# An attention backward core: q loads issued singly, the output scaled by GpSimd after one copy, and its fp32 transposes at full width

## Chip, cores and metric

The kernel runs on one core of a Trainium2 chip. The metric is the device time of one execution in microseconds (us); a kernel's figure is the median of its runs.

Engine names are those of the profile: PE is the TensorE matmul, PEld its weight load, DVE is VectorE, ACT is ScalarE, POOL is GpSimd. SP is the sync engine, which only issues DMAs here.

## The reference, cut to what matters

Two attention blocks share the input size (2048 tokens, 448 features, 16 heads of 28). Block A is linear attention, block B is softmax attention with 16 query heads over one shared k and v. The kernel returns the concatenated output and all eight gradients.

```python
def _B_ref(x, wq, wk, wv, wo):            # 16 heads, Dh = 28
    q = (x @ wq).reshape(B, S, H, Dh).transpose(0, 2, 1, 3)
    k = x @ wk
    v = x @ wv
    scores = jnp.einsum("bhqd,bkd->bhqk", q, k) * (Dh ** -0.5)
    p = softmax(scores, axis=-1)
    o = jnp.einsum("bhqk,bkd->bhqd", p, v)
    return o.transpose(0, 2, 1, 3).reshape(B, S, H * Dh) @ wo
...
def reference(A_x, ..., B_wo, grad_out):
    _out, _vjp = jax.vjp(_f, A_x, A_wqkv, A_wo, B_x, B_wq, B_wk, B_wv, B_wo)
    return (_out, *_vjp(grad_out))
```

The change touches block B alone: its forward and backward pass, which the kernel runs together in one loop.

## The kernel before

The loop, called the attention core here, has 64 blocks (a chunk of 256 queries of two heads) of 8 units (256 keys each), so 512 units. In unit u the PE makes the scores of unit u and dP of unit u-16; ACT makes two exponentials of 512 columns and one copy (`cp`) of half of dP; the DVE makes the first half of dS (`dst[:, 0, :]`) and a 32x32 transpose (`dsx`); POOL makes the other half (`dst[:, 1, :]`). A unit's number modulo 8 is its place. Once a block there is extra work for the output o:

- Place 1: the DVE copies the unnormalised o, transposed, from PSUM (`oTs`).
- Place 2: the PE transposes it into the spare PSUM bank (`onat_T`); DVE and POOL work on it (`o_norm`). Row 0 of each head holds the sum of the exponentials, so its reciprocal `rl` is one over the softmax denominator.
- Place 4: `row_D` puts sum(dO * o) into column 0 of `don`, the scaled dO.
- Place 6: the PE transposes `don` (`don_T`), again into the spare bank. From then on dP of the next block can be made.

```python
def onat_T(b, bank):
    onp = bank[:, 0:P].rearrange("p (q h c) -> p q h c", q=2, h=2)
    for qb in range(2):
        for j in range(4):
            mmt(bank[32 * j:32 * j + 32, qb * 64:qb * 64 + 64], oTs[:, qb * P + 32 * j:qb * P + 32 * j + 32],
                identF[:, 0:64], (0, 32 * j), True, True)
    onps[b] = onp

def o_norm(b):
    # ... onp, r_ (the new rl), os_ (a view of oTs), dnv (do_nat of this block)
    nc.vector.reciprocal(out=r_[:], in_=onp[:, :, :, 0:1])
    nc.vector.tensor_tensor(out=os_, in0=onp[:, :, :, :], in1=r_[:].to_broadcast([P, 2, 2, 32]), op=ALU.mult)
    # ... new tiles prod and dn (= don[b])
    nc.gpsimd.tensor_tensor(out=prod[b][:], in0=dnv, in1=os_, op=ALU.mult)
    nc.gpsimd.tensor_tensor(out=dn[:], in0=dnv, in1=r_[:].to_broadcast([P, 2, 2, 32]), op=ALU.mult)
    nc.gpsimd.tensor_copy(out=dnv, in_=os_)

def row_D(b):
    Dq = pw_.tile([P, 2, 2, 1], F32, name="Dq")
    nc.vector.tensor_reduce(out=Dq[:, :, :, 0], in_=prod[b][:], axis=AX.X, op=ALU.add)
    nc.gpsimd.tensor_tensor(out=don[b][:, :, :, 0:1], in0=Dq[:], in1=rl[b][:], op=ALU.mult)

for u in range(NU + 28):                  # NU = 512
    spare = ...                           # the score bank that unit u does not use
    rows_SD(u, sp, dp)                    # scores of u, dP of u-16
    if (b := due(u, 10)) is not None:     # place 2
        onat_T(b, spare)
    if (b := due(u, 14)) is not None:     # place 6
        don_T(b, spare)
    # ... exponential, dst[:, 0, :] on the DVE, cp on ACT, dst[:, 1, :] on POOL
    for a in {10: (0, 2), 18: (1, 3)}.get(u, ()) or {38: (0, 2), 54: (1, 3)}.get(u % 64, ()) * (u < 448):
        # ... qX[qc]: the next q chunk, a quarter (32 partitions, 256 KB) by each load
        nc.gpsimd.dma_start(qX[qc][32 * a:32 * a + 32, :, :, :]..., qn_d[qc * 256:(qc + 1) * 256, :]...)
    if u == 44:
        nc.gpsimd.dma_start(wo, ...)
    if (b := due(u, 12)) is not None:     # place 4
        row_D(b)
    # ... place 2: o_norm(b); place 6: don_copy(b); second exponential; products; dsx
```

POOL carries out its instructions in this order, so a q load issued in a unit stands ahead of `o_norm` and `row_D` of the same unit.

## Time and profile before

| | before |
|---|---|
| median of 3 runs, us | 1084.57 (1081.98 to 1086.64) |
| span of the profiled run, us; clock | 1083.6; 0.995 |
| PE, DVE, ACT, POOL busy, share of the span | 95%, 83%, 81%, 71% |
| up to the core, core (first exponential of unit 0 to that of unit 511), after it, us | 221.5, 785.5, 76.6 |
| median unit, us: place 2; place 4 (even, odd blocks); place 6 (even, odd) | 1.733; 1.596, 1.480; 1.480, 1.526 |
| median unit of an odd place, us | 1.447 |

A unit's time is read from the ACT timeline: from the start of its first exponential to that of the next unit's. The medians are over units 128 to 447, where nothing but the loop runs. I call what a unit takes above the median of its place (even and odd blocks apart) a stall, where it is over 0.1 us. Sums of stalls run over units 16 to 510 and leave out place 0, which takes 0.2 to 0.3 us more below unit 128 and from 448 on because other work falls there. Before, the stalls sum to 12.2 us.

A few more lines of before matter later. The first is from the costliest groups on the page (engine, operation, shapes, count, busy us, mean ns, idle time ahead), the second from the groups by shape between 400 and 1000 us:

```profile
L640 PE MATMUL sps<-identF,oTs 128*32 128x64 f32 x1024 | 27.6, 225 | 7.3
```
```profile
L792 POOL CAST R<-oTs 128x128 bf16<-128x128 f32 x49 | 14.2, 289 | 3.1
```

The 8 transpose products of a block are 16 MATMULs in the record (1024 in 64 blocks), and POOL's conversion of o to bf16 takes 289 ns. The waits of the PE in the core (total us, times, longest us):

```profile
PE dk_acc L640 <- issue: 3.8, 1, 3.8
...
PE sps L805 <- POOL don L797: 0.8, 1, 0.8
```

The transposes of `don` (L805) waited for POOL a single time, and the one long stall was an "issue", which is time in which the engine waited for nothing that the profile shows.

### The profile page before, as it was taken

The numbers are of one execution on the slowest core, as the hardware profiler recorded it, in microseconds if no ns is written. First come the engines' busy times: TensorE is split into PE (matmuls) and PEld (weight loads), VectorE is DVE, ScalarE is ACT, GpSimd is POOL, SyncE is SP. The second block draws the span as 40 slices with busy tenths as digits, with TensorE's granted clock in tenths as the row PEclk, the third lists the DMA queues.
The fourth block names the chain that finished last, engine by engine and source line by source line (L and its number), as shares of the span: only waits on it lengthen the run. The fifth ranks groups of instructions, "written<-read, shape, count | busy, mean of one in ns | idle before, by whom it ended". The sixth has DMA issues, their size and how long they took to land.

```text
span 1083.6 us, 41908 instructions
## 1 busy us (share of the span) xinstructions
PE 1033.1 (95%) x17222; PEld 502.1 (46%) x17225; DVE 896.5 (83%) x1790; ACT 873.4 (81%) x1743; POOL 772.4 (71%) x1014
## 2 busy tenths in 40 slices
PE   9999999999989999999999999999999999999998
PEld 5555555444434444444444444444444444444444
DVE  7896400439979999999999999999999999999942
ACT  6453122579979999999999999999999999999621
POOL 6001243328877888889889988988988898888881
PEclk9999999999999999999999999999999999999999
DMA  9879899399999999999999999999999999999973
GB/s 240 165 134 193 171 189 202 69 219 198 198 177 196 165 202 181 202 189 200 190 185 194 194 193 193 200 186 186 189 205 186 188 191 202 183 167 188 223 141 89
DMA packets 669033, 199.47 MB, mean 184 GB/s; under 512 B 646008, under 2 KB 664736, under 8 KB 668840
## 3 DMA queue, kind: packets, MB, share of 16 engines
q1 hardware_dynamic: 656296, 175.23, 96.8%
q0 software_dynamic: 7584, 17.59, 6.9%
q10 hardware_dynamic: 4960, 3.96, 1.3%
q8 instruction: 135, 2.21, 0.9%
q14 instruction: 58, 0.48, 0.1%
HBM read 20.99 MB, written 12.94 MB: 31 GB/s over the span
## 4 chain that ended last, share of the span: by engine, by line
PE 37%; ACT 25%; DVE 16%; issue 13%; POOL 6%; DMA 2%; ACTq 0%; SPq 0%; DVEq 0%; POOLq 0%
ACT cp L899 13%; PE agen L81 11%; ACT eT L932 9%; PE sps L640 7%; DVE dsx L963 6%; POOL dsT L900 5%; PE aacc L81 4%; DVE dsT L897 4%; PE oq L640 4%; PE sps L81 3%; PE dk_acc L640 2%; DVE oTs L914 2%; PE dps L640 2%; ACT eT L892 1%; DVE oTs L784 1%
## 5 line engine op out<-in xcount | busy, mean ns | idle before, releaser
L900 POOL TENSOR_TENSOR dsT<-cp,eT 128x512 bf16<-128x512 bf16 x512 | 588.2, 1156 | 107.2 <-ACT cp L899 99.8
L640 PEld LDWEIGHTS <-R 128*32 128x32 bf16 (+1 forms) x9184 | 237.6, 94 | 277.1 <-issue 242.1
L963 DVE STREAM_TRANSPOSE dsx<-dsT 128x512 f32<-128x512 f32 x512 | 357.9, 699 | 2.4 <-DVE ot L710 0.2
L897 DVE TENSOR_TENSOR dsT<-dps,eT 128x512 bf16<-128x512 f32 x512 | 342.3, 668 | 19.3 <-PE dps L640 13.8
L892 ACT ACTIVATE eT<-sps 128x512 bf16<-128x512 f32 x512 | 313.5, 612 | 28.0 <-PE dps L640 15.1
L899 ACT ACTIVATE cp<-dps 128x512 bf16<-128x512 f32 x512 | 315.6, 616 | 12.0 <-PE dps L640 10.9
L932 ACT ACTIVATE eT<-sps 128x512 bf16<-128x512 f32 x512 | 322.1, 629 | 0.0
L640 PE MATMUL dk_acc<-dsx,qX 32*32 32x512 bf16 x4096 | 269.9, 377 | 3.8 <-issue 3.8
L640 PE MATMUL dps<-doT,R 32*128 32x256 bf16 x2048 | 247.5, 269 | 2.1 <-ACT cp L899 0.8
L640 PE MATMUL sps<-R,R 32*128 32x256 bf16 (+1 forms) x2240 | 223.1, 275 | 10.8 <-DVE R L867 1.7
L640 PE MATMUL oq<-eT,R 128*32 128x256 bf16 x2048 | 158.6, 275 | 0.9 <-issue 0.9
L640 PE MATMUL oq<-dsT,R 128*32 128x256 bf16 x2048 | 156.8, 274 | 2.2 <-issue 2.1
L640 PEld LDWEIGHTS <-qX 32*32 32x32 bf16 x4096 | 79.9, 89 | 119.4 <-issue 59.3
L640 PE MATMUL dv_acc<-eN,don 128*32 128x512 bf16 x1024 | 97.8, 379 | 0.0
L81 PEld LDWEIGHTS <-R 128*128 128x128 bf16 (+1 forms) x525 | 41.7, 99 | 39.9 <-issue 10.2
L401 POOL COPY pk<-R 128x256 bf16<-128x256 bf16 x4 | 1.6, 397 | 73.1 <-DVE R L361 73.0
L553 DVE TENSOR_TENSOR osb<-R 32x512 bf16<-32x512 bf16 x4 | 1.7, 414 | 59.0 <-ACT R L550 59.0
L640 PEld LDWEIGHTS <-don 128*32 128x32 bf16 x1024 | 34.5, 97 | 0.7 <-issue 0.4
L640 PE MATMUL sps<-identF,oTs 128*32 128x64 f32 x1024 | 27.6, 225 | 7.3
L788 POOL TENSOR_TENSOR prod<-R,oTs 128x128 f32<-128x128 bf16 x64 | 27.6, 431 | 7.1 <-DVE oTs L784 7.0
L917 DVE TENSOR_SCALAR R<-oq 64x256 bf16<-64x256 f32 x64 | 27.3, 427 | 3.6 <-PE oq L640 1.6
L640 PEld LDWEIGHTS sps<-identF,oTs 128*32 128x32 f32 x1024 | 17.2, 109 | 25.1 <-ACT eT L932 24.7
(223 smaller groups left out, 997.6 us busy)
## 6 DMA issues: line engine op xcount, KB each, us to landing
qX<-qn_d POOLq DMA_DIRECT2D x32, 256.0 KB, 4.9
out_dram<-osb ACTq DMA_DIRECT2D x22, 112.0 KB
qn_d<-gaT SPq DMA_DIRECT2D x2, 1024.0 KB
eN<-eT SPq DMA_TRANSPOSE x128
xa<-in_A_x_dram SPq DMA_DIRECT2D x8, 224.0 KB
ga<-in_grad_out_dram SPq DMA_DIRECT2D x4, 448.0 KB
xa<-in_grad_out_dram POOLq DMA_DIRECT2D x4, 448.0 KB, 8.6
out_dram<-wdq POOLq DMA_DIRECT2D x8, 224.0 KB, 5.2
```

The lines of the kernel that those rows point to most:

```text
L81: nc.tensor.matmul(out_ap, lhsT=lhsT, rhs=rhs, start=start, stop=stop, tile_position=(0, 0))
L640: nc.tensor.matmul(out, lhsT=lhsT, rhs=rhs, start=start, stop=stop, tile_position=pos, skip_group_check=True)
L784: nc.vector.tensor_tensor(out=os_, in0=onp[:, :, :, :], in1=r_[:].to_broadcast([P, 2, 2, 32]), op=ALU.mult)
L788: nc.gpsimd.tensor_tensor(out=prod[b][:], in0=dnv, in1=os_, op=ALU.mult)
L892: nc.scalar.activation(out=eT(u)[:, 0, :], in_=sp[0][:, :], func=ACT.Exp, scale=scale)
L897: nc.vector.tensor_tensor(out=dst[:, 0, :], in0=dp[0][:, :], in1=ew[:, 0, :], op=ALU.mult)
L899: nc.scalar.activation(out=cp[:, :], in_=dp[1][:, :], func=ACT.Copy)
L900: nc.gpsimd.tensor_tensor(out=dst[:, 1, :], in0=cp[:, :], in1=ew[:, 1, :], op=ALU.mult)
L914: nc.vector.tensor_copy(out=oTs[0:64, :], in_=oq[0:64, 0:256])
L917: nc.vector.tensor_scalar(out=qT_B[g][64 * hp:64 * hp + 64, qc * 256:(qc + 1) * 256], in0=oq[64:128, 0:256], scalar1=scale, scalar2=None, ...
L932: nc.scalar.activation(out=eT(u)[:, 1, :], in_=sp[1][:, :], func=ACT.Exp, scale=scale)
L963: nc.vector.transpose(out=dsx[b][:, tp, :, :, :].rearrange("p h t c -> p (h t c)").bitcast(F32), in_=dsT[y][:, :, :].rearrange("p h c -> p ...
```

## The change

The intent: smaller bursts of DMA (one q load at a time in place of two, `wo` later), a spare bank that comes free sooner (the DVE first copies o out of PSUM and the scaling is left to POOL), and fewer PE instructions (2 full-width transposes in transpose mode in place of 8 tiled products). The whole diff:

```diff
--- before.py
+++ after.py
@@ -770,9 +770,8 @@
         def onat_T(b, bank):
             onp = bank[:, 0:P].rearrange("p (q h c) -> p q h c", q=2, h=2)
             for qb in range(2):
-                for j in range(4):
-                    mmt(bank[32 * j:32 * j + 32, qb * 64:qb * 64 + 64], oTs[:, qb * P + 32 * j:qb * P + 32 * j + 32],
-                        identF[:, 0:64], (0, 32 * j), True, True)
+                nc.tensor.transpose(onp[:, qb, :, :].rearrange("p h c -> p (h c)"), oTs[0:64, qb * P:(qb + 1) * P],
+                                    identF[0:64, 0:64], tile_position=(0, 0))
             onps[b] = onp
 
         def o_norm(b):
@@ -780,8 +779,8 @@
             qc, pair, g, hp = blk(b)
             r_ = pw_.tile([P, 2, 2, 1], F32, name="rl")
             os_ = oTs[:, 0:P].rearrange("p (q h c) -> p q h c", q=2, h=2)
-            nc.vector.reciprocal(out=r_[:], in_=onp[:, :, :, 0:1])
-            nc.vector.tensor_tensor(out=os_, in0=onp[:, :, :, :], in1=r_[:].to_broadcast([P, 2, 2, 32]), op=ALU.mult)
+            nc.vector.tensor_copy(out=os_, in_=onp[:, :, :, :])
+            nc.vector.reciprocal(out=r_[:], in_=os_[:, :, :, 0:1])
             rl[b] = r_
             dnv = do_nat[:, 2 * qc:2 * qc + 2, pair * 64:pair * 64 + 64].rearrange("p q (h c) -> p q h c", c=32)
             prod[b] = pw_.tile([P, 2, 2, 32], F32, name="prod", bufs=1)
@@ -789,11 +788,12 @@
             dn = pw_.tile([P, 2, 2, 32], BF16, name="don", bufs=3)
             don[b] = dn
             nc.gpsimd.tensor_tensor(out=dn[:], in0=dnv, in1=r_[:].to_broadcast([P, 2, 2, 32]), op=ALU.mult)
-            nc.gpsimd.tensor_copy(out=dnv, in_=os_)
+            nc.gpsimd.tensor_tensor(out=dnv, in0=os_, in1=r_[:].to_broadcast([P, 2, 2, 32]), op=ALU.mult)
 
         def row_D(b):
             Dq = pw_.tile([P, 2, 2, 1], F32, name="Dq")
             nc.vector.tensor_reduce(out=Dq[:, :, :, 0], in_=prod[b][:], axis=AX.X, op=ALU.add)
+            nc.gpsimd.tensor_tensor(out=Dq[:], in0=Dq[:], in1=rl[b][:], op=ALU.mult)
             nc.gpsimd.tensor_tensor(out=don[b][:, :, :, 0:1], in0=Dq[:], in1=rl[b][:], op=ALU.mult)
 
         def don_T(b, bank):
@@ -898,13 +898,13 @@
                     cp = pc_.tile([P, 512], BF16, name="cp")
                     nc.scalar.activation(out=cp[:, :], in_=dp[1][:, :], func=ACT.Copy)
                     nc.gpsimd.tensor_tensor(out=dst[:, 1, :], in0=cp[:, :], in1=ew[:, 1, :], op=ALU.mult)
-                for a in {10: (0, 2), 18: (1, 3)}.get(u, ()) or {38: (0, 2), 54: (1, 3)}.get(u % 64, ()) * (u < 448):
-                    qc = u // 64 + (u > 20)
+                for a in {10: (0,), 14: (2,), 18: (1,), 22: (3,)}.get(u, ()) or {34: (0,), 42: (2,), 50: (1,), 58: (3,)}.get(u % 64, ()) * (u < 448):
+                    qc = u // 64 + (u > 24)
                     if a == 0:
                         qX[qc] = (pqb_ if qc % 2 else pqa_).tile([P, 4, 2, 512], BF16, name="qX")
                     nc.gpsimd.dma_start(qX[qc][32 * a:32 * a + 32, :, :, :].rearrange("j b s c -> j b (s c)"),
                                         qn_d[qc * 256:(qc + 1) * 256, :].rearrange("(b j s) c -> j b (s c)", b=4, s=2))
-                if u == 44:
+                if u == 70:
                     nc.gpsimd.dma_start(wo, wo_d[:, 0:D].rearrange("(g p) c -> p g c", p=P))
                 if (b := due(u, 12)) is not None:
                     row_D(b)
```

Place 2 is where u % 8 == 2, and so are 34, 42, 50 and 58: the new loads stand ahead of `o_norm`'s POOL work in its own unit. Before, they stood at 38 and 54, place 6.

## The prediction

> **What bounds the kernel now.** I read the page first, then the stretches, the timeline of each engine in one block, and the DMA queues. Both parts of the change lie in the attention core: 64 blocks of 8 units (512 units), about 222 to 1010 us of the 1084. A unit holds three ACT instructions of 512 elements (two exponentials, one copy); the DVE makes half of dsT and a 32x32 transpose, POOL the other half.
>
> The chain of the page and two stretches (busy us of PE, PEld, DVE, ACT, POOL; clock; DMA share; GB/s):
> ```profile
> PE 37%; ACT 25%; DVE 16%; issue 13%; POOL 6%; DMA 2%; ACTq 0%; SPq 0%; DVEq 0%; POOLq 0%
> 300.00:330.00 30.00, 25.47 (x476) 11.38 (x469) 23.20 (x45) 23.30 (x48) 19.63 (x22) 0.89 1.22 176
> 600.00:700.00 100.00, 96.38 (x2002) 45.73 (x1997) 97.88 (x190) 98.82 (x200) 89.03 (x106) 1.00 1.16 193
> ```
> No engine is the bound alone: PE, DVE and ACT are all over 96% in the steady part. "Busy" hides waits there, as records overlap: ACT instructions last 0.60 to 0.66 us but start 0.477 us apart. So I measured pitches, start to start. Three make 1.43 us a unit. An odd unit takes 1.447 us, which is that floor; even units take more: 1.48, 1.73, 1.48 to 1.60 and 1.48 to 1.53 us for the unit's place 0, 2, 4, 6 in its block. A block is 12.05 us, ACT's floor 11.45. Place 2 is the one with the o transposes, so I followed it in the DVE's timeline (start, duration):
> ```profile
> 536.37 0.64 DVE L897 TENSOR_TENSOR dsT<-dps,eT 128x512 bf16<-128x512 f32 x1
> 536.97 0.18 DVE L783 RECIPROCAL rl<-sps 128x4 f32<-128x4 f32 x1
> 537.18 0.29 DVE L784 TENSOR_TENSOR oTs<-sps,rl 128x128 f32<-128x128 f32 x1
> 537.39 0.70 DVE L963 STREAM_TRANSPOSE dsx<-dsT 128x512 f32<-128x512 f32 x1
> 538.02 0.66 DVE L897 TENSOR_TENSOR dsT<-dps,eT 128x512 bf16<-128x512 f32 x1
> 538.70 0.43 DVE L917 TENSOR_SCALAR R<-oq 64x256 bf16<-64x256 f32 x1
> ```
> The spare PSUM bank is held until the product at 537.18 ends (537.47); the PE's next scores start at 537.53. But the DVE itself has no gap from 536.37 on until two units later: it is the bound of this part of the block, not the bank alone.
>
> POOL in the same block:
> ```profile
> 536.17 2.39 POOL L900 TENSOR_TENSOR dsT<-cp,eT 128x512 bf16<-128x512 bf16 x2
> 538.52 0.43 POOL L788 TENSOR_TENSOR prod<-R,oTs 128x128 f32<-128x128 bf16 x1
> 538.91 0.40 POOL L791 TENSOR_TENSOR don<-R,rl 128x128 bf16<-128x128 bf16 x1
> 539.37 0.29 POOL L792 CAST R<-oTs 128x128 bf16<-128x128 f32 x1
> 539.62 2.27 POOL L900 TENSOR_TENSOR dsT<-cp,eT 128x512 bf16<-128x512 bf16 x2
> 541.84 0.22 POOL L797 TENSOR_TENSOR don<-Dq,rl 128x4 bf16<-128x4 f32 x1
> ```
> POOL runs without a gap from 536.17 to 542.06, the end of don, which the PE transposes in the unit of place 6. There the PE waits for ACT to leave the bank anyhow. Over all steady blocks don ends 0.25 or 0.36 us before that unit's first ACT start, and the transpose starts 0.18 to 0.19 us after it: 0.38 to 0.50 us of slack.
>
> Last, what happens when don is late (POOL, then ACT), and the longest stall of the core (ACT):
> ```profile
> 289.27 0.81 POOL L908 DMA_DIRECT2D wo<-wo_d  x1
> 290.10 0.23 POOL L797 TENSOR_TENSOR don<-Dq,rl 128x4 bf16<-128x4 f32 x1
> ```
> ```profile
> 290.70 0.66 ACT L932 ACTIVATE eT<-sps 128x512 bf16<-128x512 f32 x1
> 291.68 0.60 ACT L892 ACTIVATE eT<-sps 128x512 bf16<-128x512 f32 x1 [0.32 <-PE dps L640]
> 318.86 0.60 ACT L932 ACTIVATE eT<-sps 128x512 bf16<-128x512 f32 x1
> 324.52 0.60 ACT L892 ACTIVATE eT<-sps 128x512 bf16<-128x512 f32 x1 [5.05 <-PE dps L640]
> ```
> In the first the issue of the wo load pushed don to 0.58 us after the unit's start, and the unit took 1.935 us in place of 1.480. In the second the PE stood 3.8 us "issue" in the middle of its dk products. The DMA queues tell why:
> ```profile
> q1 hardware_dynamic: 656296, 175.23, 96.8%
> q8 instruction: 135, 2.21, 0.9%
> ```
> 135 fetches of 16 KB are the PE's instructions (256 each). They come every 6 us, but before this stall 12.6 us lay between two; two q loads of 256 KB, issued together at 306.4, moved beside the e transposes from 310 to 319.
>
> **What the Trainium skill says.** "TensorEngine Tiling (Array Packing)", Restrictions: column tiling excludes the fp32 transpose mode; Key Properties: a change of tiling mode drains the PE. The trace agrees with both: the 8 products show as 16 MATMULs (1024 in all for 512), and each change of shape costs 0.2 to 0.4 us from last start to next start. "TensorE: Matmul & The Clock Gate", Terms: transpose mode is 4 times faster for fp32; nothing in this trace shows it. "DMA: Bandwidth & Descriptors", Queues, rings and completion order: each engine goes round the queues with work, a packet at a time. That fits the late fetch.
>
> **The change, part by part.**
> 1. o on the DVE. Removed: reciprocal (0.217 us to the next start) and product (0.208). Added: a copy of the same 128 fp32 elements, some 0.29 us, then a reciprocal that must wait until the copy has landed (another 0.03) and, reading SBUF, frees the DVE after an estimated 0.05 to 0.10 (durations of small operations less the 0.08 by which they overlap). 0.425 becomes 0.37 to 0.42: 0 to 0.05 a block. The bank comes free 0.2 us earlier, but the PE's next scores can then start only 0.11 earlier (its dv products start until 537.10 and the switch takes about 0.31), and two units later the DVE, whose chain is as long as before, takes that back. Gain 0 to 3 us in all.
> 2. fp32 transposes. 16 loads and 16 products of the PE took 0.25 us (536.40 to 536.65). Two full-width ones are not tiled: a weight load each, not overlapped by tiles, and one change of mode more. I estimate 0.25 to 0.40, so no gain; if the copy has to wait for them, a loss of up to 0.1 a block. I set 1 and 2 together to 0, within -4 to +6 us.
> 3. POOL. The cast becomes a product: its pitch of 0.25 becomes about 0.38 (that of the prod line), +0.13. The second small product of row_D must wait for the first: 0.22 + 0.05, +0.25 with the issue. Together don comes 0.38 later: just the slack. About 0.
> 4. The q loads. Each issue takes 0.55 us of POOL (measured from row to row). Before, pairs at places 6; POOL had recovered before the next o. Now single ones at units 34, 42, 50, 58 of 64: all at place 2, and in program order ahead of prod, don and the new product, in POOL's gapless stretch. In these blocks don ends 0.55 + 0.38 = 0.93 later, at +0.57 to +0.68 after the start of the unit of place 6. That is the case of unit 46 (+0.58, cost 0.455). 28 blocks have it (7 q chunks x 4). At 0.42 each, a little off for what the DVE gains while the PE waits: **+11.8 us**.
> 5. The same loads no longer in pairs, wo away from them. Stalls of the old core over its own medians by place, near q pairs: unit 63 with the two after it 6.7 us, units 303, 366 and 426 1.5, 22 and 26 1.0; near wo (46, 50) 1.9: 11.1 us. With half the burst a fetch is late less often; I take three quarters: **-8 us**.
> Sum: 1084.6 + 11.8 - 8 + 0 = 1088; I say 1087, as single stalls may all go.
>
> **Rivals.**
> Bank-bound: if the bank, not the DVE, sets place 2, its unit drops from 1.73 to about 1.53, 0.2 x 64 = 13 us; with part 5 and without part 4 that is 1064. For it: the scores start 0.05 us after the product ends. Against: the gapless DVE.
> Late don stays hidden: if POOL takes the loads in time, or the compiler orders them later, part 4 falls away: 1076.
> New PE cost: the untiled fp32 products take several passes and hold up the copy: 0.15 x 64 = 10 us more, 1097. Against: the tiling page gives the new form a faster mode that the old one could not use.
> DMA as it was: the stalls do not depend on pairs but on where a fetch falls; then part 5 gives nothing: 1095.
>
> **Range and chances.** The terms in doubt are 5 (0 to -11), 4 (0 to +15) and 1 with 2 (-13 to +10), mostly independent: about 12 us each way. 1075 to 1099. Faster by 2% means under 1063: the bank rival with all stalls gone and no late don, 0.04. Slower by 2% means over 1106: new stalls or slow transposes on top of part 4, 0.06.
>
> **What would show it.** In the page after: four or fewer fp32 transpose MATMULs a block; small POOL products twice as many; in the waits, PE transposes of don waiting for POOL in about 28 blocks for some 0.4 us each; ACT gaps there; place 2 near 1.7 us still; no stall over 2 us near 318. I am wrong if place 2 falls to 1.55, if don's waits do not grow, or if long "issue" stalls stand elsewhere.

## The result, and the profile after

| | before | after |
|---|---|---|
| median, us (range, 4 runs each) | 1085.46 (1081.98 to 1086.64) | 1097.17 (1092.5 to 1098.05) |
| ratio of times | | 1.0105, 95% interval 1.0067 to 1.0142 |
| span of the profiled run, us; clock | 1083.6; 0.995 | 1095.9; 0.994 |
| PE, DVE, ACT, POOL busy | 95%, 83%, 81%, 71% | 94%, 82%, 80%, 72% |
| up to the core, core, after it, us | 221.5, 785.5, 76.6 | 225.5, 793.8, 76.6 |

The kernel became 1% slower: inside the predicted range and within 2%, but 10 us above the predicted value.

The page after: the chain that ended last, and the DMA queues for data and for PE instructions (packets, MB, share).

```profile
PE 36%; POOL 28%; ACT 19%; issue 9%; DVE 5%; DMA 4%; ACTq 0%; DVEq 0%; POOLq 0%; SPq 0%
...
q1 hardware_dynamic: 656296, 175.23, 94.1%
...
q8 instruction: 128, 2.10, 0.8%
```

POOL went from 6% of the chain to 28% although its busy share moved by one point: so it hardly works more, but more of what ends last waits for it. The chain is one of several near-equal paths, so this is a pointer and not a measure. The fetches fell from 135 to 128, since there are 893 fewer MATMULs and 896 fewer weight loads. The same two stretches as in the prediction:

```profile
300.00:330.00 30.00, 26.85 (x532) 12.38 (x533) 27.59 (x53) 27.98 (x56) 26.16 (x34) 1.00 1.19 200
...
600.00:700.00 100.00, 94.26 (x1856) 42.71 (x1848) 95.93 (x186) 97.28 (x195) 89.20 (x112) 1.00 1.16 195
```

In the first the stall of before is gone (ACT busy 28 of 30 us, before 23). In the steady stretch PE, DVE and ACT are all less busy, ACT 195 instructions in place of 200: this part became slower. Which units became slower, from the differences of each unit's time (after less before):

| units | number | difference, us |
|---|---|---|
| place 6 of the blocks with a q load | 28 | +14.65 |
| units 0 to 33 | 34 | +6.16 |
| place 6 of the other blocks | 32 | +0.38 |
| place 2 | 60 | -7.72 |
| units 63 to 65 (the long stall of before) | 3 | -6.40 |
| all others | 354 | +1.23 |
| **core** | 511 | **+8.3** |

The other 4.0 us of the span's 12.3 lie ahead of the core, in code that is the same in both kernels. In the 13 profiles that stretch takes 221.2 to 225.9 us, without regard to the kernel; it is chance.

**Place 6.** A block with a q load, on POOL:

```profile
581.79 0.58 POOL L905 DMA_DIRECT2D qX<-qn_d  x1
582.39 0.44 POOL L787 TENSOR_TENSOR prod<-R,oTs 128x128 f32<-128x128 bf16 x1
582.78 0.40 POOL L790 TENSOR_TENSOR don<-R,rl 128x128 bf16<-128x128 bf16 x1
583.26 0.40 POOL L791 TENSOR_TENSOR R<-oTs,rl 128x128 bf16<-128x128 f32 x1
...
585.84 0.21 POOL L796 TENSOR_TENSOR Dq<-Dq,rl 128x4 f32<-128x4 f32 x1
586.12 0.22 POOL L797 TENSOR_TENSOR don<-Dq,rl 128x4 bf16<-128x4 f32 x1
```

and what the PE and then ACT did there (in brackets the idle time ahead and what ended it):

```profile
586.39 0.23 PE L805 MATMUL sps<-identB,don 128*32 128x128 bf16 x2 [0.70 <-POOL don L797]
```
```profile
587.69 0.60 ACT L892 ACTIVATE eT<-sps 128x512 bf16<-128x512 f32 x1 [0.46 <-PE dps L640]
```

The load takes POOL 0.58 us and comes first, then the three products, two products of dS, and two small products in place of one. `don` is done at 586.34, the PE starts its transposes 0.05 later, after 0.70 us of idleness, and ACT's first exponential of the next unit comes at 587.69, 2.06 us after this unit's (585.63), where 1.48 is usual. Over all such blocks the median unit takes 2.041 us (even) and 2.155 (odd). In the waits of the core this is the top line by far:

```profile
PE sps L805 <- POOL don L797: 22.3, 41, 0.8
PE dk_acc L640 <- DMA qX<-qn_d: 2.9, 1, 2.9
```

**Units 0 to 33.** The second line is a new wait: `dk_acc` at unit 27 is the first user of the first q chunk, and the last quarter of it, now issued at unit 22, had not landed. On ACT:

```profile
270.94 0.60 ACT L892 ACTIVATE eT<-sps 128x512 bf16<-128x512 f32 x1 [4.15 <-PE dps L640]
```

**Place 2.** The DVE in unit 210, which starts at 555.50 (the prediction shows unit 202 of before, which starts at 536.21; the figures of before below are those of its unit 210, at 548.21):

```profile
555.66 0.64 DVE L897 TENSOR_TENSOR dsT<-dps,eT 128x512 bf16<-128x512 f32 x1
556.23 0.27 DVE L782 COPY oTs<-sps 128x128 f32<-128x128 f32 x1
556.53 0.18 DVE L783 RECIPROCAL rl<-oTs 128x4 f32<-128x4 f32 x1
556.63 0.69 DVE L963 STREAM_TRANSPOSE dsx<-dsT 128x512 f32<-128x512 f32 x1
557.23 0.66 DVE L897 TENSOR_TENSOR dsT<-dps,eT 128x512 bf16<-128x512 f32 x1
```

From the unit's start the copy begins at 0.735 us (before, the reciprocal at 0.763), copy and reciprocal take 0.395 to the next start (0.426), and the next dS starts at 1.736 (1.814): the DVE won 0.08 us, and the unit takes 1.653 in place of 1.733. The PE's next scores start at 1.230 instead of 1.325.

The groups by shape, 400 to 1000 us, for the transposes and POOL's last product:

```profile
L773 PE MATMUL sps<-identF,oTs 64*128 64x64 f32 x98 | 16.4, 248 | 5.8
...
L791 POOL TENSOR_TENSOR R<-oTs,rl 128x128 bf16<-128x128 f32 x48 | 19.2, 399 | 3.8
```

There are two MATMULs a block in place of 16. In that unit the PE starts its next work 0.461 us after the unit's start, before 0.442, so the PE itself won nothing, although its last transpose starts 0.10 us earlier in the unit (0.308 for 0.406): before, the tiled products were followed by products of the same tiling 0.036 us after the last start, and now 0.153 us pass there.

### The profile page after: what moved, and what is told of

Read it like the earlier page. It is cut to its first block, busy times and chain, and to the rows that moved or that the text cites. A ratio compares the mean times of both kernels' runs of the same rounds, so it can differ in the third digit from the quotient of the medians.

```text
span 1095.9 us, 40183 instructions
## 1 busy us (share of the span) xinstructions
PE 1031.4 (94%) x16329; PEld 486.2 (44%) x16329; DVE 894.5 (82%) x1790; ACT 876.7 (80%) x1743; POOL 788.9 (72%) x1078
## 4 chain that ended last, share of the span: by engine, by line
PE 36%; POOL 28%; ACT 19%; issue 9%; DVE 5%; DMA 4%; ACTq 0%; DVEq 0%; POOLq 0%; SPq 0%
POOL dsT L900 18%; PE agen L81 12%; ACT cp L899 10%; ACT eT L932 6%; PE sps L640 6%; PE aacc L81 4%; PE oq L640 4%; PE sps L81 3%; POOL prod L787 2%; POOL R L791 2%; POOL don L790 2%; PE dv_acc L640 1%; PE dk_acc L640 1%; PE dps L640 1%; DMA eN<-eT 1%
## 5 line engine op out<-in xcount | busy, mean ns | idle before, releaser
L640 PEld LDWEIGHTS <-R 128*32 128x32 bf16 (+1 forms) x9184 | 225.3, 94 | 278.3 <-issue 237.2
L805 PE MATMUL sps<-identB,don 128*32 128x128 bf16 x256 | 18.5, 223 | 25.2 <-POOL don L797 22.3
L791 POOL TENSOR_TENSOR R<-oTs,rl 128x128 bf16<-128x128 f32 x64 | 25.6, 399 | 5.0
```

What stands on the lines that cost most here:

```text
L640: nc.tensor.matmul(out, lhsT=lhsT, rhs=rhs, start=start, stop=stop, tile_position=pos, skip_group_check=True)
L791: nc.gpsimd.tensor_tensor(out=dnv, in0=os_, in1=r_[:].to_broadcast([P, 2, 2, 32]), op=ALU.mult)
```

## The experiments

**The main theory.** `don` had 0.38 to 0.50 us of slack. The new POOL work of o and the issue of a load together are more than that in 28 blocks, and what exceeds it lengthens the unit of place 6 one to one. Neither alone would do much harm. **Rivals:** the transfer of the load, not its issue, holds things up; the o work alone is the cause; the stalls near loads follow from pairs or from chance. The experiments are diffs to the kernel before or after, all correct, each timed against before on the same chip.

### e1: the loop's loads back at place 6

```diff
 # against after
-{34: (0,), 42: (2,), 50: (1,), 58: (3,)}
+{38: (0,), 46: (2,), 54: (1,), 62: (3,)}
```

> The changed kernel with the 28 single q loads of the loop moved from place 2 to place 6 of their blocks (units 38, 46, 54, 62 of 64), all else kept. Theory A (the loads' issue stands on POOL ahead of the o work and makes don late): the unit of place 6 in those blocks falls from 2.04 to 2.15 us back to 1.48 to 1.58, PE waits for don fall from 22 us to a few, and the run gets 14 us faster than the changed kernel, to about 1083. Rival B (single loads hurt wherever they stand, by their transfers): place 6 or another place stays about 0.5 us longer in those blocks and the run stays near 1096.

Measured: 1081.07 us, before 1086.51, ratio 0.9969 (0.9927 to 1.0010). Place 6 is 1.480 and 1.581 in blocks with a load, as in those without. The wait for `don`:

```profile
PE sps L805 <- POOL don L797: 5.8, 28, 0.3
```

What is left, 28 waits of 0.2 us on average, falls into the odd blocks, whose place 6 is 0.055 us longer than before. The place of the issue is the cause of the 0.56 and 0.63 us. The core is 16.3 us shorter than after's (777.5), which is what the 28 units cost there. The stall of unit 27 remains (4.1 us).

### e2: the loads alone, e3: the work of o alone

```diff
 # e2: before, with after's two lines of the load schedule and wo at 70
 # e3: after, with before's load schedule and wo at 44
```

> The kernel before with the new load schedule alone (q loads and wo). Theory A with the slack of 0.38 to 0.50 us that the prediction measured: the loads alone make don late by 0.55, of which the slack takes most, so place 6 of the 28 blocks is only 0.06 to 0.2 us longer, 2 to 5 us in all; with the stalls the run is within 1083 to 1092. Rival C (the loads cost their 0.5 us a block without any help of the o work): place 6 at 2.0 and the run near 1098.

> The changed kernel with the old load schedule (pairs at places 6, wo at unit 44). Theory A: don comes 0.38 later in every block and just fits; place 2 at 1.65 instead of 1.73, place 6 at 1.48 and 1.58, so 3 to 5 us faster than before, about 1081, if the stalls are those of before. Rival D (the added POOL work costs by itself): place 6 above 1.7 in all 64 blocks and a run over 1090.

Measured: e2 1086.86 (ratio 1.0018, 0.9976 to 1.0061), e3 1079.85 (0.9963, 0.9918 to 1.0008), before 1086.51 in both. The table has the end of `don` and the start of its first transpose from the first exponential of the unit of place 6, and that unit's time, as medians, even/odd blocks:

| kernel, blocks | don ends, us | transposes start, us | unit, us |
|---|---|---|---|
| before | -0.36 / -0.25 | 0.18 / 0.19 | 1.480 / 1.526 |
| e2 (loads), with a load | 0.21 / 0.32 | 0.26 / 0.38 | 1.560 / 1.676 |
| e3 (o), all | 0.11 / 0.23 | 0.18 / 0.28 | 1.480 / 1.582 |
| after, without a load | 0.11 / 0.23 | 0.18 / 0.28 | 1.480 / 1.580 |
| after, with a load | 0.69 / 0.80 | 0.74 / 0.86 | 2.041 / 2.155 |

The load makes `don` 0.57 us later, the o work 0.47, both 1.05: they add. The unit's time doesn't: alone they cost 0.08 and 0.15 (e2) or 0 and 0.06 (e3), together 0.56 and 0.63. Once the transposes wait for `don`, the unit ends 1.30 us after they start, in every row (0.26 + 1.30 = 1.56, 0.74 + 1.30 = 2.04). So `don` may come 0.49 us later (even) or 0.42 (odd) before the unit gets longer: 0.57 - 0.49 = 0.08, 1.05 - 0.49 = 0.56. That is a slack which either part alone about uses up and both together overrun, and the rival that the o work alone is the cause falls.

e2 also has a stall that no theory foresaw, of 4.2 us at unit 67:

```profile
PE sps L640 <- issue: 3.6, 1, 3.6
```

and e3 one of 5.1 us at unit 52, where the PE waited 4.3 us for a DMA transpose of the exponentials.

### e4: the first chunk in pairs again

```diff
 # against after
-{10: (0,), 14: (2,), 18: (1,), 22: (3,)}
+{10: (0, 2), 18: (1, 3)}
```

> The changed kernel with the first chunk's loads in pairs at units 10 and 18 as before, the rest new. Theory E (the stalls at units 20 and 27 of the changed kernel, 6 us, come from the last first-chunk load being issued 5 units before its first use): they go and the run gets about 6 us faster, 1091. Rival F (such stalls come from a late instruction fetch or a saturated DMA and only move): units up to 70 together lose about as much as in the changed kernel, and the run stays within 2 us of 1097.

Measured: 1090.81, before 1086.51, ratio 1.0062 (1.0017 to 1.0108). Unit 27 has no stall; place 6 is as in after (2.040 and 2.154). The stall at unit 27 is thus bound to the issue at unit 22. It is in all five profiles in which the last quarter of the first chunk is issued there (after, e1, e2, e7, e10: 2.9 to 7.5 us) and in none of the eight in which it is issued at 18 or 14. The prediction hadn't looked at that: in after the load was issued at 259.85 and the PE ran out of work at 265.55.

### e5: copy alone, e6: transposes alone

```diff
 # e5: before, with after's o_norm and row_D (copy, reciprocal, scaling on POOL)
 # e6: before, with after's onat_T only
-                for j in range(4):
-                    mmt(bank[32 * j:32 * j + 32, ...], oTs[:, ...], identF[:, 0:64], (0, 32 * j), True, True)
+                nc.tensor.transpose(onp[:, qb, :, :]..., oTs[0:64, qb * P:(qb + 1) * P], identF[0:64, 0:64], ...)
```

> The kernel before with o's copy and the scaling on GpSimd, but its 8 tiled products and its old loads. If the gain at place 2 (1.733 to 1.653 us) comes from the shorter DVE chain and the bank freed one instruction earlier, nearly all of it is here: place 2 at 1.65 to 1.68, don 0.47 later than before, 3 to 5 us faster than before less stalls. If it comes from the transposes, place 2 stays at 1.73.

> The kernel before with o's full-width transposes alone. Their last product ended 0.09 us earlier in the changed kernel but the next work of the PE began 0.02 later. If only the DVE's earlier start counts, the reciprocal moves 0.03 earlier and place 2 falls to about 1.70, 2 us in all; if the transposes bring the gain, place 2 is at 1.65; if nothing, 1.73. don as before (0.25 and 0.36 before the unit's start).

Measured, against before at 1082.39: e5 1083.38, ratio 0.9994 (0.9945 to 1.0044); e6 1075.40, ratio 0.9912 (0.9873 to 0.9952). Median units:

| kernel | place 2 | place 4, even / odd | place 6, even / odd | sum of the three, mean of even and odd |
|---|---|---|---|---|
| before | 1.733 | 1.596 / 1.480 | 1.480 / 1.526 | 4.774 |
| e5 (copy) | 1.635 | 1.654 / 1.526 | 1.480 / 1.551 | 4.741 |
| e6 (transposes) | 1.683 | 1.596 / 1.480 | 1.480 / 1.525 | 4.724 |
| e3 (both) | 1.653 | 1.598 / 1.481 | 1.480 / 1.582 | 4.724 |

With the copy alone place 2 loses 0.10 us, and place 4, two units later, takes 0.05 of it back, as the prediction argued for the DVE, whose next dS starts only 0.04 us earlier (1.776 for 1.812 from the unit's start). The transposes alone win 0.05 a block (3.2 us in 64) and give nothing back. Both together win no more than the transposes alone, because the o work makes `don` late in odd blocks. How the transposes win it is in the PE's and the DVE's groups of e6:

```profile
L773 PE MATMUL sps<-identF,oTs 64*128 64x64 f32 x98 | 16.4, 247 | 5.8
...
L782 DVE RECIPROCAL rl<-sps 128x4 f32<-128x4 f32 x49 | 7.8, 159 | 0.2 <-issue 0.2
```

The reciprocal that follows them takes 159 ns, after the tiled products 182; the copy takes 267 ns in after and 291 in e5. It isn't the way in which the bank was filled: in before, units 26 and 178, whose tiled products ended 0.31 us or more ahead of the reciprocal, have 157 and 159 ns, and in e6, units 18 and 426, where the DVE had stood idle just before, have 182 and 183. The short form goes with products that were done early, the long one with a DVE that had to wait. The last transpose starts 0.405 us into the unit in before and 0.307 in e6. The reciprocal starts at 0.761 us in before and takes 0.218 to the next start; in e6 it starts at 0.736 and takes 0.193. The two differences are the 0.05 us. That the earlier end of the transposes brings them is read from the traces; no run moved that end alone.

The bank is free 0.05 us earlier with that (the product ends at 1.270 and 1.221), and the PE's next scores follow 0.05 after it in both kernels (1.323 and 1.273): there the bank sets the end of place 2. With the copy it is free at 1.04 (e5) and 1.00 (after), but the scores start at 1.210 and 1.229 only, so the bank is no longer what they wait for.

The ratio of e6 is better than 3.2 us explain (3.2 of 1082 is 0.3%, the ratio says 0.9). Its stalls sum to 5.3 us in place of 12.2, which is the rest in this profile. How large the stalls of the runs without a profile were isn't on record; their spread is below.

### e7: the loads issued by the sync engine

```diff
 # against after
-nc.gpsimd.dma_start(qX[qc]...
+nc.sync.dma_start(qX[qc]...
```

> The changed kernel with the q loads issued by SyncE in place of GpSimd, at the same units. Theory A (the cost is the time of the issue on POOL): don ends at +0.23 and +0.11 of the unit of place 6 in all blocks, place 6 is 1.48 and 1.58 everywhere, 14 us faster than the changed kernel apart from stalls (the loads now queue behind the e transposes, so stalls can grow). Rival B (the transfer at that moment costs): place 6 stays at 2.04 and 2.15 in the 28 blocks.

Measured: 1082.82, before 1082.39, ratio 0.9980 (0.9943 to 1.0018). The loads move the same bytes and stand at the same units of the program, but POOL has no issue to carry out, and place 6 is 1.480 and 1.584 as in blocks without a load. It is POOL's issue time that counts, not the transfer. The Trainium skill, "Perfetto Trace Analysis", DMA Optimizations, advises to spread DMAs over the engines that can issue them where descriptor generation is the bottleneck; the trace agrees (0.56 us saved in each even block with a load, 0.57 in each odd one). It has a price, however:

```profile
PE dk_acc L640 <- DMA qX<-qn_d: 6.2, 1, 6.2
PE sps L805 <- POOL don L797: 6.1, 29, 0.3
```

The stall of unit 27 is the longest (7.5 us). The sync engine also issues the DMA transposes, and the load stood behind one:

```profile
258.64 5.06 SPq L934 DMA_TRANSPOSE eN<-eT  x1
263.75 0.58 SPq L905 DMA_DIRECT2D qX<-qn_d  x1
```

Unit 22, to which this load belongs, starts at 253.78, and the PE starts its last product before the stall at 261.60, ahead of the load's issue.

### e8: a version meant to beat both, and e9: the first chunk earlier

```diff
 # e8, against e1: first chunk in pairs at 10 and 18, and one small product fewer
-nc.gpsimd.tensor_tensor(out=prod[b][:], in0=dnv, in1=os_, op=ALU.mult)      # ahead of dn
+nc.gpsimd.tensor_tensor(out=prod[b][:], in0=dn[:], in1=os_, op=ALU.mult)    # after dn, which has rl in it
-nc.gpsimd.tensor_tensor(out=Dq[:], in0=Dq[:], in1=rl[b][:], op=ALU.mult)
 # e9, against e8
-{10: (0, 2), 18: (1, 3)}
+{10: (0, 2), 14: (1, 3)}
```

> A version meant to beat both: the changed kernel with the loop's q loads at place 6, the first chunk's in pairs at 10 and 18, and the product for D made from the scaled do (don times o), so that row_D needs one small product again. Theory A: don ends some 0.25 us earlier than in the changed kernel's plain blocks, below the 0.13 that costs, so place 6 is 1.48 and 1.53; place 2 stays 1.65. With stalls of 3 to 11 us the run takes 1073 to 1081.

> The version meant to beat both, with the second pair of the first chunk's loads at unit 14 (place 6) in place of 18 (place 2). Theory A also holds there: the 1.4 us that unit 22 lost to a late don goes, all else as in that version, so 1 to 2 us faster than it: about 1073. Rival: the earlier megabyte only brings another stall of the kind that the other runs show between units 20 and 70, and nothing is gained.

Measured: e8 1074.97, before 1082.39, ratio 0.9903 (0.9860 to 0.9946); e9 1077.18, before 1085.65, ratio 0.9932 (0.9893 to 0.9970). In e8 `don` ends 0.28 us earlier (even blocks) than in after's blocks without a load, and place 6 of odd blocks is back at 1.528. The second small product (e8 also swaps the order of `prod` and `dn`) thus cost 0.05 us in each odd block and nothing in the even ones. In e9 unit 22, whose stall in the kernels with pairs at 18 is 0.7 to 2.2 us, stalls by only 0.3; but unit 20 stalled 4.8 us for another transfer:

```profile
PE dv_acc L640 <- DMA eN<-eT: 4.1, 1, 4.1
```

so nothing was won.

### e10: after again, and e11: e8 again

> The changed kernel once more, for a comparison in the same rounds and a second profile. Units of place 6 in the 28 blocks at 2.04 and 2.15 again, as they repeat in every block; the stalls before unit 70 and the start of the core (225.5 us in its first profile, 221.3 to 225.9 in the others, whose code up to there is the same) are expected to differ, if they are chance. About 1096.

> The version meant to beat both once more in the same rounds: 1075, about 1% below the kernel before and 2% below the changed one; place 2 at 1.65, place 6 at 1.48 and 1.53; only the stalls differ from its first profile.

Measured, both against before at 1085.65: e10 1096.65, ratio 1.0111 (1.0072 to 1.0149); e11 1074.55, ratio 0.9905 (0.9870 to 0.9940). Both repeat: after is 1.1% slower than before, e8 1% faster than before. In e10 the 28 units of place 6 are 14.87 us longer than before's (after: 14.65), place 2 is 7.97 shorter (7.72) and unit 27 stalls again. The stalls of the two profiles of e8, the same kernel, sum to 6.1 and 1.8 us: a sum of stalls has to differ by more than some 4 us from another before it says anything. From unit 34 on, the sums are 11.2, 8.8, 7.2 and 3.5 us in the four profiles with the loop's loads in pairs and `wo` at 44 (before, e3, e5, e6) and 0.5 to 6.9, on average 2.3, in the nine with single loads and `wo` at 70.

## Why the prediction was right or wrong

The class was right and the time inside the range, but the sum it rested on was +3.8 us, and the span rose by 12.3. That the time stayed inside the range is in part luck: without the 4.8 us that place 2 won against the prediction it would have been 1102. By its steps:

- **Part 4, the loads: the mechanism was right, a term of its sum was too small.** PE transposes of `don` wait for POOL in the 28 blocks, as named. The 28 units of place 6 are 16.2 us above before's medians (14.65 above the same units of before, which had 1.5 us of stalls in them), not 11.8. The mis-sized term is the cost of a block, put at 0.42 us; it is 0.56 in even blocks and 0.63 in odd ones. Two things made it so. `don` was late by 1.05 us more, not 0.93: the issue costs 0.57 (0.55 predicted), the o work 0.47 (0.38 predicted). (Unit 46, from which the cost was taken, is in an odd block, whose usual time is 1.526 us and not 1.480: there it had cost 0.41 and not 0.455.) And the deduction "for what the DVE gains while the PE waits" hardly came: the other places of these blocks have the medians of blocks without a load, except place 0 of odd blocks with 1.481 for 1.493.
- **Part 3, POOL: the work was sized right, the slack was not.** The delay was put at 0.38, "just the slack", and at no cost. POOL's extra work was that: the two small products start 0.28 us apart, and the product takes 399 ns where the cast took 289, so 0.39. But measured from the unit that needs `don` the delay is 0.47, because that unit now comes 0.08 earlier: POOL runs from place 2 on at its own pace, while place 2 became 0.08 shorter. e6 shows this term alone: there POOL's work is as before, place 2 is 0.05 shorter, and `don` ends 0.05 later against its unit (-0.32 and -0.20 for -0.36 and -0.25). Odd blocks, with the lesser slack, pay 0.055 us each, 0.9 us in the 16 of them without a load.
- **Parts 1 and 2: put at 0, measured -0.08 us at place 2, 4.8 us in 60 units.** The step that failed is that the full-width transposes bring "no gain". It was worked out from the PE's time, and there it is right: from the first transpose to the PE's next work 0.265 us pass, before 0.247. But the last transpose starts 0.10 us earlier, and the DVE's next instruction on the bank starts 0.025 earlier and is shorter, 159 for 182 ns (e6), as if it no longer had to wait. Part 1's own estimates held: copy and reciprocal take 0.395 us (0.37 to 0.42 predicted), with the copy alone the scores start 0.11 earlier (0.11 predicted), and the DVE takes back what the bank yields (e5: 0.10 won at place 2, 0.05 lost at place 4). The rest of place 2's -7.72 us are stalls of before at units 50, 178, 370, 450 and 458 (2.9 us).
- **Part 5, stalls: -8 predicted, -3.3 measured** (12.2 to 8.9), less than two profiles of one kernel differ by. From unit 34 on they fell by 9.7 (11.2 to 1.5), near the -8; up to unit 33 they rose by 6.4 (1.0 to 7.4). The stall at unit 63 did go, with the two units after it, 6.4 us. That the loads in pairs caused it isn't shown: e3 and e6 keep them and have no stall there. What failed is that only the loop's loads were looked at: the first chunk's last load was moved four units nearer to its first use and created a new stall, 4.3 us at unit 27. That is shown by e4. That single loads cause fewer late fetches is not shown: the stalls from unit 34 on are smaller on average with them (2.3 for 7.7 us), but the ranges overlap, `wo` was moved too, and e2 has single loads and an issue stall of 3.6 us at unit 67.
- **Ahead of the core:** +4.0 us in the two profiles, chance, in no part of the prediction.

16.2 - 3.3 - 4.8 + 0.9 is +9.0, near the +8.3 that the core shows; most of the 0.7 left over is unit 64, which lost 0.6 us before and is of place 0, left out of the sums of stalls.

**The rivals.** Bank-bound: right for before, where the scores start 0.05 us after the bank is free, but place 2 did not fall to 1.53: with the copy the scores no longer wait for the bank, and it is 1.653, 0.08 of the 0.2. Late `don` hidden: no. New PE cost: no; place 2 fell. DMA as it was: open, see part 5. The prediction's list of signs was right on the MATMUL count (2 a block), the small products (twice as many), the waits for `don` (41, 22.3 us) and the missing stall near 318; it was wrong by 0.05 us on place 2, and a long stall elsewhere did come up, though by "DMA", not by "issue".

**Open.** Why stalls of 2 to 5 us fall at unit 20, 52, 62 or 67 in single runs and what makes the stretch ahead of the core 221 or 226 us. The versions e6 (one part of the change, 1075.4 us) and e8 (all of it, moved and trimmed, 1075.0 and 1074.6) are not told apart: by their medians e8 should be 0.027 us a block better, 1.7 us in 64.

## What to carry to other kernels

Slack is shared. Before work is put on an engine with in-order issue, find the consumer that waits for its last result, measure how early that result is today, and sum everything in the change that delays it, a DMA's issue time on that engine included: two delays of 0.47 and 0.57 us that cost 0.15 us or less each cost 0.6 together against a slack of 0.4 to 0.5, and whatever makes the consumer come sooner takes from the same slack. And when a load is moved, look at the time from its issue to its first use, above all for the first pass of a loop, where nothing is ahead.

## What the Trainium skill lacked or had wrong

- "DMA: Bandwidth & Descriptors", Anatomy of one DMA, fits a DMA issued by GpSimd as 2.0 us plus the bytes at 436 GB/s and doesn't say how long GpSimd itself is held. By that fit a q load of 256 KB should land after 2.6 us, an estimate; here the median is 4.9 us before and 4.1 after, beside DMA queues that are busy all the time. The issue holds GpSimd for 0.57 to 0.58 us (579 ns on average in after's steady part), and that was the largest single cost of this change.
- "TensorEngine Tiling (Array Packing)", Key Properties, says that a change of tiling mode drains the PE, without a figure. Here 0.153 us pass from the last start of the full-width transposes to the next products, where tiled ones of the same mode as their followers left 0.036.
- "TensorE: Matmul & The Clock Gate", Terms, has transpose mode 4 times faster for fp32. The runs show one MATMUL a product in place of two and 2 products in place of 8, but one record takes 248 ns, against 225 for a tiled one. The last transpose starts 0.10 us earlier in the unit, and the PE's next work 0.02 later.
- No page that I read says that the record of one and the same DVE instruction differs in length with whether it had to wait: 182 and 159 ns for the reciprocal (before, e6), 291 and 267 for the copy (e5, after). That the wait makes the difference is inferred, from units 26 and 178 of before and 18 and 426 of e6.
- "Runtime: NRT & Kernel Launch", Instruction fetch mechanics, doesn't give what a late fetch of PE instructions looks like in a profile. What fits one here: in before, a stall of 3.8 us labelled "issue", with 12.6 us between two fetches that otherwise come every 6 us. A gap alone is no proof: 11.0 us at unit 410 of after went with a stall of 0.2 us.
